# Expert layers as a 3x2 by 2x3 block product in 15 products, with the order written by a list scheduler

## The chip, the cores and the metric

The kernel runs on one core of a Trainium2 chip. The core has a matrix engine, TensorE (PE in the profile; PEld is its loading of weights), and three engines for element-wise work: VectorE (DVE), ScalarE (ACT) and GpSimd (POOL). A fifth, SyncE (SP), issues transfers. The engines run side by side, each through its own instructions in their written order, and wait for one another by semaphores. Matrix results land in PSUM, eight banks of 512 fp32 values in each of 128 partitions; everything else works in SBUF.

The metric is the device time of one launch in microseconds (us), lower is better.

## The reference

A state-space block (Mamba-2) is followed by four experts whose outputs are mixed with given weights. All is fp32.

```python
# x: (4, 8, 768, 32), a: (4, 8, 768), B and C: (4, 8, 768, 16), in chunks
L = np.exp(cum[:, :, :, None] - cum[:, :, None, :]) * causal
M = np.einsum('bhin,bhjn->bhij', Cc, Bc) * L
y[:, :, sl] = einsum(M, xc) + einsum(Cc, state) * decay_to_i
state = decay_full * state + sum(Bc * xc * decay_from_j)
...
# N, D, E, F = 3072, 256, 4, 1024; x is y turned to (3072, 256)
p = domain_probs / (domain_probs.sum(-1, keepdims=True) + 1e-09)
for e in range(E):
    h = np.maximum(x @ w1[e], 0.0)
    out += p[:, e:e + 1] * (h @ w2[e])
```

By far most of the arithmetic is in the two matrix products of the experts.

## The kernel before

**Chunks and blocks.** The 3072 tokens are 24 chunks of 128. Six blocks of 512 tokens (four chunks, one of each sequence) go through the experts one after the other; the hidden units of all experts are eight steps of 512 per block, so there are 48 steps `n`. While one block is in the experts, the scans, scores and outputs of the next block's four chunks are worked in between: `decay_part` (scans on DVE, line L364), `masks` (ACT), `scores` (PE, L393), `masked` (DVE, L405), `outputs` (PE, L450 and L462; ACT copies them to `yT`), `carry` (DVE, the state).

**Seven products for eight.** In a step each layer is a 2x2 by 2x2 block product: 256 tokens x 128 inputs against 256 hidden units, computed in seven block products after Strassen and Winograd. One block product is two matmuls of 128x128 weights against 128x256 tokens; the profile shows it as four matmul records. `fmul` (L523) does the first layer, `smul` (L608) the second. Steps 0 and 1 are done plainly, eight products a layer (`plain_first` L572, `plain_second` L589). The price of seven products is sums: of weights (`sums_of`, POOL, L189 to L193, once per step and then kept in HBM as `w1_d` and `w2_d`), of tokens (`sums`, DVE, L501 to L504, once per block), of first-layer results (`snap`, an ACT copy, L530; `total`, DVE, L535), and of gated hidden values (`diff`, DVE, L552). `gated` (DVE, L545) takes the maximum with zero and multiplies by the expert's weight.

**Second-layer sums stay in PSUM.** Four banks (`acc0` to `acc3`) hold the seven products of a block and are added to over all eight steps. After the last, `keep` and `combine` turn them into the output, which `turned_out` and `leave` write. Two banks (X, Y) serve the first layer and two the attention.

**Order.** All is written out by hand: the step loop interleaves the first layer of step n with the second layer of step n-1, and puts the attention's parts between at fixed places. Loads are issued by SP, in its one queue; the stores of weight sums by POOL:

```python
def sums_of(op, part):
    if part != 1:
        nc.gpsimd.tensor_add(op(S1), op(S3), op(A22))
...
            nc.gpsimd.dma_start(out=w1_d[n], in_=wt1[n][:, S3:])
```

Of the kernel before, what the change touches and what calls it, by code (L numbers as in the profile page):

```python
# [8 lines left out]
FP32 = mybir.dt.float32  # L9
# [3 lines left out]
P = 128  # L13
NQ, NT = 4, 2


@with_exitstack
def kernel(
# [10 lines left out]

# [3 lines left out]
    E, DM, F = w1.shape  # L60
    NH = NQ * NT
    HN = P
    BLK = 512
    HB = BLK // 2
    CPB = BLK // P
# [5 lines left out]
    FH = F // 2  # L71
    JJ = FH // HB
    SPB = E * JJ
    NS = NBLK * SPB
    assert NBLK == chunks_per_seq

    def real(c):

        return c % CPB * NBLK + c // CPB

    PLAIN = 2
    A12, A22, A11, S3, S1, S2, S4 = range(7)

    const = ctx.enter_context(tc.tile_pool(name="const", bufs=1))
    load = ctx.enter_context(tc.tile_pool(name="load", bufs=3))
    wts = ctx.enter_context(tc.tile_pool(name="wts", bufs=3))
    att = ctx.enter_context(tc.tile_pool(name="att", bufs=2))
    ffn = ctx.enter_context(tc.tile_pool(name="ffn", bufs=2))
    ps_att = ctx.enter_context(tc.tile_pool(name="ps_att", bufs=2, space=bass.MemoryType.PSUM))
    ps_f = ctx.enter_context(tc.tile_pool(name="ps_f", bufs=1, space=bass.MemoryType.PSUM))  # L90
    ps_s = ctx.enter_context(tc.tile_pool(name="ps_s", bufs=1, space=bass.MemoryType.PSUM))
    ctx.enter_context(tc.manual_schedule())


    ac_d = tc.dram_tile([NCH, NH, P], FP32, name="ac_d")
    acut_d = tc.dram_tile([NCH, NH, P], FP32, name="acut_d")
    p_d = tc.dram_tile([T // P, E, P], FP32, name="p_d")
    w1_d = [tc.dram_tile([P, 4, HB], FP32, name=f"w1_d{i}") for i in range(SPB)]
    w2_d = [tc.dram_tile([P, 5 * HB], FP32, name=f"w2_d{i}") for i in range(SPB)]


    st = {}
    SPREAD = 3

    HALF = P // 2

    def turned_round(c):


        return c >= CPB and c % 2 == 1  # L110

    def load_tokens(c):
        xb = load.tile([P, W], FP32, tag="xb", name="xb", bufs=4)
        src = xbc[real(c)]
        if turned_round(c):
            nc.sync.dma_start(out=xb[:, :OBT], in_=src[:, :OBT])
            nc.sync.dma_start(out=xb[:HALF, OBT:], in_=src[HALF:, OBT:])
            nc.sync.dma_start(out=xb[HALF:, OBT:], in_=src[:HALF, OBT:])
        else:
            nc.sync.dma_start(out=xb, in_=src)  # L120
        st.setdefault(c, {})["xb"] = xb

    def load_rows(c):

        xb = load.tile([P, W], FP32, tag="xb", name="xb", bufs=4)
        nc.sync.dma_start(out=xb[:, OBT:], in_=xbc[real(c)][:, OBT:])
        st.setdefault(c, {})["xb"] = xb

    def load_rest(c):
        nc.sync.dma_start(out=st[c]["xb"][:, :OBT], in_=xbc[real(c)][:, :OBT])  # L130

    def load_decays(c):
        ab = load.tile([P, NH * P], FP32, tag="ab", name="ab")
        nc.sync.dma_start(
            out=ab, in_=acut_d[real(c)].rearrange("h s -> (h s)").partition_broadcast(P))
        st.setdefault(c, {})["ab"] = ab

    def load_heads(c):

        ah = st[c]["ah"] = load.tile([HN, P], FP32, tag="ah", name="ah", bufs=4)  # L140
# [7 lines left out]
    def load_chunk(c):  # L148
        load_tokens(c)
        load_decays(c)  # L150
        load_heads(c)

    wt1, wt2 = {}, {}

    def load_w1(n):
        e, jj = divmod(n % SPB, JJ)
        t1 = wt1[n] = wts.tile([P, 7, HB], FP32, tag="wt1", name="wt1", bufs=5)
        for k in range(2):
            w = 2 - 2 * k
            a_ = 2 if n < SPB or k else 1  # L160
            nc.sync.dma_start(
                out=t1[:, w:w + a_],
                in_=w1[e, k * P:k * P + P].rearrange("p (a f) -> p a f", a=2)[
                    :, 0:a_, jj * HB:jj * HB + HB])
        if n >= SPB:
            nc.sync.dma_start(out=t1[:, S3:], in_=w1_d[n % SPB])

    def load_w2(n):
        e, jj = divmod(n % SPB, JJ)
        t2 = wt2[n] = wts.tile([P, 7 * HB], FP32, tag="wt2", name="wt2", bufs=5)  # L170
        for i in range(2) if n < SPB else (1,):
            f = i * FH + jj * HB
            nc.sync.dma_start(
                out=t2[:, (1 - i) * 2 * HB:(2 - i) * 2 * HB].rearrange("p (j m) -> p j m", j=JJ),
                in_=w2[e, f:f + HB].rearrange("(j p) m -> p j m", p=P))
        if n >= SPB:
            nc.sync.dma_start(out=t2[:, 2 * HB:], in_=w2_d[n % SPB])

    def w2_op(n, w):

        if w < 4:
            a_, d = divmod(w, 2)
            return wt2[n][:, :4 * HB].rearrange(
                "p (a j d m) -> p a j d m", a=2, j=JJ, d=2)[:, a_, :, d]
        return wt2[n][:, w * HB:w * HB + HB].rearrange("p (j m) -> p j m", j=JJ)

    def sums_of(op, part):
        if part != 1:
            nc.gpsimd.tensor_add(op(S1), op(S3), op(A22))  # L189
            nc.gpsimd.tensor_sub(op(S2), op(S1), op(A11))  # L190
            nc.gpsimd.tensor_sub(op(S4), op(A12), op(S2))
        if part != 0:
            nc.gpsimd.tensor_sub(op(S3), op(A11), op(S3))  # L193

    def sum_w1(n, part=None):


        if n < SPB:
            sums_of(lambda w: wt1[n][:, w].rearrange("p (j m) -> p j m", j=JJ), part)
            if part != 0:  # L200
                nc.gpsimd.dma_start(out=w1_d[n], in_=wt1[n][:, S3:])

    def sum_w2(n, part=None):
        if n < SPB:
            sums_of(lambda w: w2_op(n, w), part)
            if part != 0:
                nc.gpsimd.dma_start(out=w2_d[n], in_=wt2[n][:, 2 * HB:])

    pr = const.tile([P, T // P, E], FP32, name="pr")
    a_sb = const.tile([NCH * NH // 2, 2, P], FP32, name="a_sb")  # L210

    a_q = ffn.tile([P, SPREAD, NT, P], FP32, tag="o", name="a_q", bufs=1)
    nc.gpsimd.memset(a_q[:, 0], 0.0)
    one = nc.const_aps.tensor(1.0, [P, 1])
    nc.vector.memset(a_q[:, 1:], 0.0)
    nc.scalar.dma_start(out=pr, in_=probs)
    for queue, c in ((nc.sync, slice(0, 1)), (nc.scalar, slice(1, SPREAD))):
        queue.dma_start(
            out=a_q.rearrange("(q r) c t s -> q r c (t s)", q=NQ)[:, 0, c],
            in_=a.rearrange("(i k) (q t) s -> k q i (t s)", k=NBLK, t=NT)[0][:, c])  # L220
    warm = const.tile([P, 1], FP32, name="warm")
    nc.scalar.mul(warm, one, one)
    load_rows(0)
    nc.sync.dma_start(
        out=a_sb, in_=a.rearrange("c h s -> (c h) s").rearrange("(p r) s -> p r s", r=2))
    load_rows(1)
    load_rest(0)
    load_rest(1)
    load_w1(0)
    load_tokens(2)  # L230

# [14 lines left out]

# [4 lines left out]

# [8 lines left out]

    def clip_first(engine, c):
        clip(engine, a_q[:, c].rearrange("p c t s -> p (c t s)"), own)
        engine.memset(a_q[:, c, :, 0:1], 0.0)

    clip_first(nc.vector, slice(0, 1))


# [705 lines left out]
```

## Time and profile before

| | |
|---|---|
| median of 3 runs | 638.26 us (637.63 to 638.26) |
| span of the profiled execution, first to last instruction | 636.4 us |
| PE busy | 631.9 us (99%), 3405 matmul records |
| DVE busy | 483.4 us (76%) |
| ACT busy | 119.7 us (19%) |
| POOL busy | 112.9 us (18%) |
| transfers | 121.61 MB, mean 191 GB/s |

The page gives no other time of the profiled execution than its span; the median of the runs is 1.9 us above it. A group line names the kernel's line, the engine, the operation, what it writes and reads, and its shapes; then how often, the busy time and the mean of one. A timeline line begins with the start from the span's beginning and the length, both in us; the brackets at its end give idle time before it and what ended that. Matmuls are pipelined: a record is 0.38 us long, and the next starts 0.216 us after it.

By stage, the busy time of each engine:

| stretch, us | PE | DVE | ACT | POOL |
|---|---|---|---|---|
| 0 to 13.28 (start, first chunks) | 12.15 | 9.30 | 5.99 | 9.26 |
| 13.28 to 60 | 46.72 | 37.97 | 7.53 | 36.69 |
| 60 to 160 | 100.00 | 85.47 | 19.59 | 36.81 |
| 160 to 400 | 240.00 | 186.64 | 45.00 | 17.63 |
| 400 to 631 | 231.00 | 162.54 | 40.55 | 10.46 |

### The profile page before, as it was taken

Reading aid. Unit: us, or ns where it says so; the run is one execution under the profiler, and the core shown is the slowest. Engines: PE = TensorE matmul, PEld = TensorE weight load, DVE = VectorE, ACT = ScalarE, POOL = GpSimd, SP = SyncE. Lnnn points to the kernel's source line nnn. Section 1 sums busy time; section 2 is a strip of 40 time slices with the busy share of each in tenths; the row PEclk is TensorE's granted clock in tenths of the full one; section 3 lists DMA queues with packets and bytes.
Section 4 is the critical chain, followed back from the end, with each engine's and each line's share of the span. In section 5 each row is a group of like instructions: output and inputs, shape, how many; then the busy total and the mean of one; then the engine's idle time right before and its main releaser. Section 6 shows DMA issues by size and latency. Waiting matters only on the chain.

```text
span 636.4 us, 9259 instructions
## 1 busy us (share of the span) xinstructions
PE 631.9 (99%) x3405; PEld 538.2 (85%) x3405; DVE 483.4 (76%) x810; ACT 119.7 (19%) x264; POOL 112.9 (18%) x164
## 2 busy tenths in 40 slices
PE   9999999999999999999999999999999999999997
PEld 5888888888888888888888888888888888888886
DVE  7868999887787788678687778778867677756555
ACT  4011221212111221122211221122111211111110
POOL 6788557020000002000002000000100000100001
PEclk9999999999999999999999999999999999999999
DMA  6998894745666392757284566639365644167001
GB/s 188 302 357 295 282 346 156 279 169 166 191 200 238 90 366 81 228 175 248 99 287 149 168 199 196 231 102 358 89 220 162 242 160 133 61 152 241 2 1 33
DMA packets 98513, 121.61 MB, mean 191 GB/s; under 512 B 29529, under 2 KB 81957, under 8 KB 98469
## 3 DMA queue, kind: packets, MB, share of 16 engines
q1 hardware_dynamic: 95512, 111.20, 53.7%
q0 software_dynamic: 2432, 9.50, 3.8%
q8 instruction: 27, 0.44, 0.3%
q10 hardware_dynamic: 524, 0.32, 0.2%
q14 instruction: 18, 0.14, 0.1%
HBM read 108.16 MB, written 12.83 MB: 190 GB/s over the span
## 4 chain that ended last, share of the span: by engine, by line
PE 99%; ACT 0%; DVE 0%; issue 0%
PE acc L608 44%; PE X L523 25%; PE Y L523 19%; PE acc L589 2%; PE g L393 2%; PE y L462 2%; PE X L572 1%; PE Y L572 1%; PE y L450 1%; PE t L729 1%; PE a L331 0%; PE y L428 0%; PE gp L309 0%; PE turned L655 0%; DVE o L686 0%; ACT p_sb L298 0%
## 5 line engine op out<-in xcount | busy, mean ns | idle before, releaser
L535 DVE TENSOR_TENSOR z<-Y,snap 128x512 f32<-128x512 f32 x138 | 94.6, 686 | 117.6 <-ACT snap L530 66.7
L608 PE MATMUL acc<-hT,wt 128*128 128x256 f32 x736 | 181.1, 379 | 0.0
L530 ACT COPY snap<-X 128x512 f32<-128x512 f32 x138 | 80.8, 586 | 464.2 <-PE X L523 403.5
L608 PEld LDWEIGHTS acc<-hT,wt 128*128 128x128 f32 x736 | 140.1, 190 | 18.7
L608 PE MATMUL acc<-h,wt 128*128 128x256 f32 x552 | 142.6, 381 | 0.0
L523 PE MATMUL X<-yS,wt 128*128 128x256 f32 x552 | 141.8, 380 | 0.0
L608 PEld LDWEIGHTS acc<-h,wt 128*128 128x128 f32 x552 | 104.2, 190 | 16.8 <-issue 2.3
L523 PEld LDWEIGHTS X<-yS,wt 128*128 128x128 f32 x552 | 105.0, 190 | 14.3 <-issue 0.3
L545 DVE SCALAR_TENSOR_TENSOR h<-z,gate 128x512 f32<-128x512 f32 x138 | 99.9, 724 | 3.5 <-PE acc L589 0.4
L523 PE MATMUL Y<-yT,wt 128*128 128x256 f32 x368 | 94.5, 379 | 0.0
L523 PEld LDWEIGHTS Y<-yT,wt 128*128 128x128 f32 x368 | 68.9, 190 | 10.5
L552 DVE TENSOR_TENSOR hT<-h,hT 128x512 f32<-128x512 f32 x92 | 65.2, 709 | 1.8
L552 DVE TENSOR_TENSOR hT<-h,h 128x512 f32<-128x512 f32 x92 | 65.1, 748 | 1.4
L364 DVE TENSOR_TENSOR_SCAN LT<-ab,ident 128x512 f32<-128x512 f32 x42 | 52.1, 1242 | 0.0
L523 PE MATMUL Y<-yS,wt 128*128 128x256 f32 x184 | 48.3, 385 | 0.0
L523 PE MATMUL X<-yT,wt 128*128 128x256 f32 x184 | 47.3, 379 | 0.0
L369 POOL TENSOR_TENSOR MT<-xb,LT 128x128 f32<-128x128 f32 x20 | 8.6, 428 | 205.4 <-PE Y L523 68.8
L405 DVE TENSOR_TENSOR MT<-g,LT 128x256 f32<-128x256 f32 x93 | 32.0, 415 | 11.5 <-PE g L393 11.4
L523 PEld LDWEIGHTS Y<-yS,wt 128*128 128x128 f32 x184 | 34.2, 190 | 6.4 <-issue 2.2
L523 PEld LDWEIGHTS X<-yT,wt 128*128 128x128 f32 x184 | 35.0, 190 | 4.7
L545 DVE SCALAR_TENSOR_TENSOR h<-X,gate 128x512 f32<-128x512 f32 x50 | 34.2, 684 | 5.0 <-PE X L523 3.4
L350 POOL TENSOR_TENSOR cts<-ctm,dec 128x256 f32<-128x256 f32 x20 | 14.1, 726 | 128.3 <-DVE dec L347 128.3
(103 smaller groups left out, 325.2 us busy)
## 6 DMA issues: line engine op xcount, KB each, us to landing
wt<-in_w_dram SPq DMA_DIRECT2D x112, 256.0 KB
wt<-w_d SPq DMA_DIRECT2D x40, 640.0 KB
wt<-w_d SPq DMA_DIRECT2D x40, 512.0 KB
ab<-acut_d SPq DMA_DIRECT2D x21, 512.0 KB
gate<-p_d SPq DMA_DIRECT2D x23, 256.0 KB
w_d<-wt POOLq DMA_DIRECT2D x8, 640.0 KB, 3.7
wt<-in_w_dram SPq DMA_DIRECT2D x40, 128.0 KB
w_d<-wt POOLq DMA_DIRECT2D x8, 512.0 KB, 7.7
```

What stands on the lines that cost most here:

```text
L350: nc.gpsimd.tensor_mul(cts, s["ctm"], dec.unsqueeze(1).to_broadcast([HN, NT, P]))
L364: nc.vector.tensor_tensor_scan(out=LT[:, i * w:i * w + w], data0=s["a"][i], data1=ident.rearrange("p h s -> p (h s)")[:, :w], initial=0.0, ...
L393: nc.tensor.matmul(out=g.rearrange("p t s -> p (t s)"), lhsT=s["xb"][k, OBT:OBT + P], rhs=s["ctm"][k].rearrange("p t s -> p (t s)"), start ...
L405: nc.vector.tensor_mul(s["MT"][:, h, 0:P], s["g"][q], s["LT"][:, h])
L462: nc.tensor.matmul(out=y[32 * q:32 * q + 32, t, 0:w], lhsT=s["xb"][:, h * D:h * D + D], rhs=s["MT"][:, NT * q + t, 0:w], start=(k == 0 and ...
L523: nc.tensor.matmul(out=f[bank][:, j], lhsT=wt1[n][:, w, j * P:j * P + P], rhs=rhs, start=(i in (1, 2, 5) and j == 0), stop=(j == JJ - 1), ...
L530: nc.scalar.copy(out=s, in_=first[n]["X"])
L535: nc.vector.tensor_add(z, first[n]["Y"], first[n][i])
L545: nc.vector.scalar_tensor_tensor(out=h, in0=first[n][src], scalar=0.0, in1=g.unsqueeze(1).to_broadcast([P, JJ, HB]), op0=ALU.max, op1=ALU. ...
L552: nc.vector.tensor_sub(h[o], h[x], h[y])
L572: nc.tensor.matmul(out=f[bank][:, j], lhsT=wt1[n][:, w, j * P:j * P + P], rhs=yT[k][:, i, cols], start=(i == 0 and j == 0), stop=(i == 1), ...
L608: nc.tensor.matmul(out=acc[k, u][:, half], lhsT=w2_op(n, w)[:, j], rhs=rhs[:, j], start=(begins and j == 0), stop=(n % SPB == SPB - 1 and ...
```

## The change

**The product.** A block is now 768 tokens (six chunks), so there are four. Hidden units come in 16 slices of 256, over the expert boundaries. A *group* is three slices: its first layer is a 3x2 by 2x3 block product (three slices, two halves of the 256 inputs, three pieces of 256 tokens), done in 15 block products in place of 18 (`group_first`); its second layer is 15 in place of 18 too (`group_second`). Five groups are 15 slices; the 16th is done plainly (unit "R"). Block 0 does four slices plainly and has four groups. The tables `SUMS`, `TOKENS`, and the code of `group_first`, `group_right` and `result` are the sums around the 15 products.

**Second-layer sums.** There are 15 sums and the plain slice's extra two, more than the banks hold. They live in SBUF tiles and visit PSUM two at a time (`visit`): ACT copies the pair into a bank, four matmuls (two products) add to it, ACT copies it back.

**Weight sums.** Ten per layer and group, stored in HBM in pairs, by SP, and loaded again in later blocks. They, and every sum with both inputs in SBUF, may be done by DVE or POOL; `ASIDE0` and `ASIDE1` name sums that only POOL may do, in block 0 and in the other blocks.

**Order and buffers.** Nothing after the start is written in its final order. Each piece of work is put in a `Plan` with a duration per engine, what it reads and writes; only PE's order is given (`line`: the second layer of the last unit alternates with the first layer of this one, with scores and outputs of two chunks after the first and the 14th piece). `Plan.run` then walks through time, gives each engine in turn the ready work that is most urgent, assigns the buffer, and the instructions are emitted in the order of the planned starts. It runs while the program is built; on the chip the order is fixed, and waits follow real times.

```diff
+HOP = 0.2
+LANDING = 2.2
+KEEP = 5
+NV, NW = 33, 32
+ASIDE0 = ("t67", "p", 2, 11)
+ASIDE1 = ("t67", "p", 2, 11, "d", 7, 6, 5, 8, 12, 3)
+SC, OUT = 1, 14
...
+            e = min(t, key=lambda e: t[e])
+            now = t[e]
+            best, soon = None, None
+            late = self.late = max(0.0, t["PE"] - line[head].nominal) if head < len(line) else 0.0
+            for w in waiting[e]:
+                if w.start is not None or e == "PE" and w.place != head:
+                    continue
+                ready = max([w.ready] + [
+                    n.end + (0.0 if n.by == e and e != "SP" else HOP) for n in w.needs])
+                if len(w.on) > 1 and e == "POOL":
+                    end = max(ready, now) + w.on[e]
+                    if end > w.latest + late + w.on["DVE"] - 1.0:
+                        queue = sum(x.on["DVE"] for x in waiting["DVE"]
+                                    if x.start is None and x.latest <= w.latest)
+                        if end > max(now, t["DVE"]) + queue:
+                            continue
+                if best is not None and ready <= now and w.latest >= best[0]:
+                    continue
+                when, homes = self.homed(w, max(now, ready))
+                if when is None:
+                    continue
+                if when <= now + 0.02:
+                    if best is None or w.latest < best[0]:
+                        best = w.latest, w, when, homes
+                elif soon is None or when < soon:
+                    soon = when
...
+BLOCKS = {3: (0, 0), 9: (0, 1), "b": (1, 0), 13: (1, 1), 7: (2, 0), 0: (2, 1)}
+SUMS = ((12, "b", 13), (2, "b", 7), (11, 12, 7), (5, 11, 0), (10, 3, 12), (8, 10, 9),
+        (1, 8, 0), (6, 1, 7), (14, 5, 9), (4, 3, "b"))
+TOKENS = (("e", (0, 2), (0, 0), -1), (11, "e", (1, 2), -1), ("g", (1, 2), (1, 0), -1),
+          (2, (1, 2), (0, 2), -1), (13, "g", "e", -1), (6, (0, 0), (0, 1), 1),
+          (3, 6, (0, 2), -1), (10, "e", (1, 1), -1), (14, (1, 2), 6, -1), (4, (1, 1), (0, 1), -1),
+          (1, 6, (1, 1), -1), (9, (1, 1), "g", -1))
+RIGHT = {0: (1, 0), 5: (1, 2), 7: (0, 0), 8: (1, 1), 12: "e"}
+FIRST = (7, 12, 5, 11, 0, 3, 2, 10, 6, 13, 8, 14, 4, 1, 9)
+SECOND = ((13, 2), (11, 4), (0, 7), (1, 14), (6, 9), (5, 8), (10, 12), (3,))
+PAIRS = {1: ((12, 5), (11, 2), (10, 6), (8, 14), (4, 1)),
+         2: ((2, 11), (4, 1), (14, 6), (5, 8), (10, 12))}
...
+    homes = {
+        "V": some(NV, [P, 2, FB], "v"),
+        "W": some(NW, [P, 2 * FB], "w"),
+        "bank": some(8, [P, 512], "bank", psum),
...
-    def sums_of(op, part):
-        if part != 1:
-            nc.gpsimd.tensor_add(op(S1), op(S3), op(A22))
-            nc.gpsimd.tensor_sub(op(S2), op(S1), op(A11))
-            nc.gpsimd.tensor_sub(op(S4), op(A12), op(S2))
-        if part != 0:
-            nc.gpsimd.tensor_sub(op(S3), op(A11), op(S3))
...
+
+    plan = Plan(homes)
+    line = []
+    B512, B256 = {"DVE": .73, "POOL": 1.65}, {"DVE": .42, "POOL": .78}
...
+    def dma(fn, n=1, kb=256, **kw):
+        return plan.add({"SP": .38 * n}, fn, lag=LANDING + kb / 190, **kw)
...
-    def fmul(n, i):
...
+    def product(bank, half, w, x, start):
+
         for j in range(JJ):
+            o = bank.rearrange("p (a m) -> p a m", a=2)[:, j if half is None else half]
             nc.tensor.matmul(
-                out=f[bank][:, j], lhsT=wt1[n][:, w, j * P:j * P + P], rhs=rhs,
-                start=(i in (1, 2, 5) and j == 0), stop=(j == JJ - 1), skip_group_check=True)
-
...
+    def combine(x, y, sign=1, reuse=None, name=None):
+
+        v = value("V")
+        engines = {"POOL": B512["POOL"]} if name in aside_of[0] else B512 if "bank" not in (x.kind, y.kind) else {"DVE": .7}
+        if reuse is None:
+            reuse = x if x.kind == "V" else y
+        plan.add(engines, lambda e: (on(e).tensor_add if sign > 0 else on(e).tensor_sub)(
+            flat(v), whole(x), whole(y)), reads=[x, y], writes=[v], reuse=reuse)
+        return v
...
+    def group_weights(k, g):
+
+        for l, load, half in ((1, load_w1, w1_half), (2, load_w2, w2_half)):
+            where = {}
+            for f in range(3):
+                v = value("W")
+                dma(lambda e, load=load, v=v, f=f: load(1 + 3 * g + f, v.t), part=[v])
+                for r, b in BLOCKS.items():
+                    if b[0] == f:
...
+                    where[r] = v, j
+                if (g, l, i) in stored:
+                    dma(lambda e, v=v, i=i, l=l: nc.sync.dma_start(out=v.t, in_=w_d[g, l, i]),
+                        part=[v])
...
+                for r, x, y in SUMS:
+                    plan.add(B256, lambda e, r=r, x=x, y=y, view=view: on(e).tensor_add(
+                        view(r), view(x), view(y)), reads=[where[x][0], where[y][0]],
+                        part=[where[r][0]])
+                for i, pair in enumerate(PAIRS[l]):
+                    v = where[pair[0]][0]
+                    dma(lambda e, v=v, i=i, l=l: nc.sync.dma_start(out=w_d[g, l, i], in_=v.t),
+                        reads=[v], due=lambda v=v: v.readers[-1])
+                    stored.add((g, l, i))
+            weights[k, g, "where", l] = where
+            weights[k, g, "view", l] = view
...
+    def group_first(k, g):
+
+        seq = []
+        where, view = weights[k, g, "where", 1], weights[k, g, "view", 1]
+        G = [gate_of(k, 1 + 3 * g + f) for f in range(3)]
+        h, z, s, bank = {}, {}, {}, {}
+
+        def mul(r, into=None):
+            y, at = tokens[k, r]
+            b = into or value("bank")
+            seq.append(plan.add({"PE": .863}, lambda e: product(
+                b.t, None, view(r), at(y), into is None), reads=[where[r][0], y], writes=[b]))
+            return b
+
+        def gate(f, n, x):
+            h[f, n] = gated(x, G[f], n, -1 if f == 1 else 1)
+
+        for r in FIRST:
+            if r == 7:
+                bank[7] = mul(7)
+                s[7] = snap(bank[7])
+            elif r in (12, 5):
+                s[r] = snap(mul(r))
+                if r == 5:
+                    q = combine(s[5], s[12], -1, reuse=False)
+            elif r == 11:
+                mul(11, bank[7])
+                z[2, 2] = combine(bank[7], q, reuse=q)
+                gate(2, 2, z[2, 2])
+            elif r == 0:
+                b = mul(0, seed(s[7]))
+                gate(2, 0, b)
+            elif r == 3:
+                bank[3] = mul(3)
+                s[3] = snap(bank[3])
+            elif r == 2:
+                mul(2, bank[7])
+                z[1, 2] = combine(bank[7], s[12], -1)
+                gate(1, 2, z[1, 2])
+            elif r == 10:
+                mul(10, bank[3])
+                v17 = combine(bank[3], s[12], -1)
+            elif r == 6:
+                bank[6] = mul(6)
+                s[6] = snap(bank[6])
+                t67 = combine(s[6], s[7], -1, name="t67")
+            elif r == 13:
+                mul(13, bank[7])
+                gate(1, 0, bank[7])
+            elif r == 8:
+                bank[8] = mul(8)
+                z[0, 1] = combine(bank[8], v17)
+                gate(0, 1, z[0, 1])
+            elif r == 14:
+                mul(14, bank[6])
+                f19 = combine(bank[6], s[5], -1)
+                u = combine(f19, z[0, 1], -1, reuse=z[0, 1])
+                z[0, 2] = combine(f19, s[3], -1, name="z02")
+                gate(0, 2, z[0, 2])
+            elif r == 4:
+                b = mul(4, seed(v17))
+                gate(1, 1, b)
+            elif r == 1:
+                mul(1, bank[8])
+                z[2, 1] = combine(t67, bank[8], -1)
+                gate(2, 1, z[2, 1])
+            elif r == 9:
+                b = mul(9, seed(u))
+                gate(0, 0, b)
+        return seq, h
+
+    def group_right(h):
+
+        n10, n11, n12 = h[1, 0], h[1, 1], h[1, 2]
+        T = {13: n10, 4: n11, 1: h[2, 1], 0: h[2, 0], 9: h[0, 0]}
+        T[2] = combine(n10, n12, name=2)
+        p = combine(h[2, 2], n12, name="p")
+        T[11] = combine(p, n10, reuse=False, name=11)
+        d = combine(h[2, 0], h[2, 1], -1, name="d")
+        T[7] = combine(d, T[11], name=7)
+        T[14] = combine(h[0, 0], h[0, 2], name=14)
+        T[6] = combine(h[2, 1], T[14], name=6)
+        x9 = combine(h[0, 1], h[0, 0], -1, name="x9")
+        T[5] = combine(h[2, 2], T[14], -1, name=5)
+        T[8] = combine(x9, h[2, 1], -1, name=8)
+        T[10] = combine(x9, n11, name=10)
+        T[12] = combine(p, T[10], name=12)
+        T[3] = combine(T[10], h[0, 2], -1, name=3)
+        return T
 
     kept = {}
...
+    def visit(k, house, terms, last=False):
+
+        seq = []
+        held = kept.get((k, house))
+        both = len({t[0] for t in terms}) == 2 or held is not None and held.both
+        bank = seed(held, len(house) * FB) if held is not None else value("bank", fills=both)
+        begun = held is not None
+        for which, w, view, x in terms:
+            half = house.index(which)
+            seq.append(plan.add({"PE": .863}, lambda e, half=half, view=view, x=x, begun=begun: product(
+                bank.t, half, view(), x.t, not begun), reads=[w, x], writes=[bank]))
+            begun = True
...
+        v.both = both
+        if both:
+            act(.6, lambda e: nc.scalar.copy(out=flat(v), in_=bank.t), reads=[bank], writes=[v])
...
+    def group_second(k, g, T):
+        where, view = weights[k, g, "where", 2], weights[k, g, "view", 2]
+        seq = []
+        for house in SECOND:
+            seq += visit(k, house, [
+                (r, where[r][0], lambda r=r: view(r), T[r]) for r in house])
+        return seq
...
+        def sum_(x, y, sign, o, part=False):
+
+            vs = dict.fromkeys((x[0], y[0]))
+            engines = B256 if all(v.kind != "bank" for v in vs) else {"DVE": .42}
+            plan.add(engines, lambda e: (on(e).tensor_add if sign > 0 else on(e).tensor_sub)(
+                o[1](), x[1](), y[1]()), reads=[v for v in vs if v is not o[0]],
+                **{"part" if part else "writes": [o[0]]})
...
+    units = [(k, g) for k in range(NBLK) for g in ([*range(NG), "R"] if k else range(1, NG))]
...
+        aside_of[0] = ASIDE0 if k == 0 else ASIDE1
...
+        merged = put(behind, seq)
...
+                scores(cs)
+                at[SC] = line[mark:]
...
+                outputs(cs)
+                at[OUT] = line[mark:]
...
+    done = plan.run(line, now, {"PE": now, "DVE": now - .6, "ACT": now + 1.0, "POOL": now - 2.0,
+                                "SP": now + .4})
+    for w in done:
+        w.fn(w.by)
```

## The prediction

> **What bounds the kernel now.** I read the first two parts of the page first: who is busy, and whether anything is ever slack.
>
> ```profile
> span 636.4 us, 9259 instructions
> ...
> PE 631.9 (99%) x3405; PEld 538.2 (85%) x3405; DVE 483.4 (76%) x810; ACT 119.7 (19%) x264; POOL 112.9 (18%) x164
> ...
> PE   9999999999999999999999999999999999999997
> ...
> DVE  7868999887787788678687778778867677756555
> ...
> POOL 6788557020000002000002000000100000100001
> ```
>
> TensorE (PE) is full in every slice, the first and last apart; VectorE (DVE) is nearly full in slices 5 to 7, where GpSimd (POOL) also works. Then the chain that ended last, in order of time, to see what a product costs and how the kernel ends:
>
> ```profile
> 621.83 0.86 PE Y L523 x4
> 622.69 0.86 PE X L523 x4
> 623.55 7.77 PE acc L608 x36
> ```
>
> Four matmul records are one product (two 128x128x256 matmuls, two records each): 0.863 us. In the page's groups L523 and L608 have 1288 records each, L572 and L589 64 each: 2704/4 = 676 products, 583.4 us. The products start at 13.28 and end near 632.4, with 0.9 us of transposes among the last: 618.2 us, of which 34.8 is not products. That is scores, outputs and spreads of 22 chunks, about 1.57 each, with no room left for stalls. So there are two questions: how many products go, and whether PE stays fed.
>
> The third view decides the second question. It is the timeline of POOL, then of DVE, in one stretch where both work on SBUF, and DVE again where POOL rests:
>
> ```profile
> 92.81 0.73 POOL L189 TENSOR_TENSOR wt<-wt 128x256 f32<-128x256 f32 x1
> 93.62 1.06 POOL L190 TENSOR_TENSOR wt<-wt 128x256 f32<-128x256 f32 x1
> 94.77 1.06 POOL L191 TENSOR_TENSOR wt<-wt 128x256 f32<-128x256 f32 x1
> 95.79 1.17 POOL L193 TENSOR_TENSOR wt<-wt 128x256 f32<-128x256 f32 x1
> ```
>
> ```profile
> 92.64 1.46 DVE L545 SCALAR_TENSOR_TENSOR h<-z,gate 128x512 f32<-128x512 f32 x1
> 94.03 2.35 DVE L552 TENSOR_TENSOR hT<-h,hT 128x512 f32<-128x512 f32 x2
> 96.78 0.69 DVE L535 TENSOR_TENSOR z<-Y,snap 128x512 f32<-128x512 f32 x1 [0.41 <-ACT snap L530]
> ```
>
> ```profile
> 109.08 1.41 DVE L552 TENSOR_TENSOR hT<-h,hT 128x512 f32<-128x512 f32 x2
> ```
>
> The two sums of L552 take 1.41 alone and 2.35 beside POOL; POOL's sum takes 0.73 alone and 1.06 to 1.17 beside them. Their ends alternate, about 0.55 us for DVE's turn and 0.6 for POOL's. The z sum that reads PSUM keeps its 0.69.
>
> [...] here a 128x256 sum takes 0.724 against 0.415.
>
> **PE, part by part.** New blocks of 768 tokens, four of them. A group is three 256-wide slices of hidden units: 15 products in the first layer and 15 in the second, in place of 18 and 18. 16 slices are five groups and one plain slice (12 products). Block 0 takes four slices plainly: 48 + 4 x 30 = 168. Blocks 1 to 3: 5 x 30 + 12 = 162 each. Sum 654. So 22 products go: -22 x 0.863 = -19.0 us. The product's shape, the scores and outputs (22 chunks after the start) and the start up to 13.2 are as before: 0. The end: after the last product two 0.42 sums, two turns of PE (0.45 for two transposes in the chain before), a copy (0.37) and a transfer, as now, but one DVE sum more in a row: +0.5. Base: 636.4 - 19.0 + 0.5 = 617.9 of span; the median stands 1.9 over the span, so 619.8 if nothing stalls.
>
> **ACT.** Second-layer sums now leave PSUM after each visit and return: eight houses a group, a seed and a copy of 128x512 (0.586) each, 9.2 us; first layer five snaps and three seeds, 4.7. With masks and copies of two chunks (about 2.4) 16.3 of a unit's 29.1 us (30 products are 25.9, plus 2 x 1.57). Hidden behind PE as long as a bank is free: a visit is 0.59 + 1.73 + 0.59 plus hops, some 3.5 us, and eight banks share it with the first layer. The seed, a copy from SBUF into PSUM, is not in the trace: the copy the other way is its price, and ACT's spare 12 us a unit would bear it at nearly twice that. New waits: a product into a seeded bank waits for ACT, one that adds to a bank already read (11, 2, 13, 10, 14, 1) for ACT or DVE; all later products stand behind it on PE's queue. I take 0 to 4 us over the run; without the cover, 16 copies a unit at 0.59 would be 9 us a unit.
>
> **DMA.** Per group 6 loads of 256 KB, and from block 1 on 10 stored sums of 256 KB: 4 MB in 25.9 us, 155 GB/s, with two chunks (0.9 MB each) and the gates about 225; slices of the page reach 366. Stores (50 of 256 KB) move from POOL's queue, where an issue took POOL 0.6 us (16 of them), to SP's. SP issues some 600 transfers; the 522 of before took 0.51 each with their waits, so it is busy half the time. In SP's one queue a store waiting for a sum holds the loads behind it; these have one unit of lead (32 tiles hold two groups). Cost 0 to 3, I take 1 with ACT's.
>
> **DVE and POOL, the dear part.** Per group, first layer: 6 sums reading PSUM, 9 gates (4 read PSUM), 3 SBUF sums, plus t67 on POOL; second layer 13 SBUF sums, 10 forced to POOL in blocks 1 to 3 (ASIDE1), 3 in block 0 (ASIDE0). Neighbouring DVE starts are 0.61 (independent) to 0.72 apart: 0.65 taken. A 128x512 sum on POOL is not in the trace; 128x128 takes 0.413 and 128x256 0.724, so another 256 gives 1.35 (estimate; [...] twice 0.724 = 1.45 is the other end). The plan counts 1.65 for it and 0.73 for a DVE sum: averages that know nothing of turns.
>
> Blocks 1 and 2, a unit with two chunks (29.1 us): DVE 21 x 0.65 + four scans of 1.13 + eight masks of 0.33 + decay and carry 2.2 = 23.1. POOL 11 x 1.35 + 2.2 = 17.1. Turns: DVE 11 x 0.55 + 4 x 1.05 + 1 = 11.3, POOL about 15; 26 of 29 us for one lock. DVE waits whenever it comes to an SBUF sum while POOL holds the lock, roughly half of 19 times, 0.65 us: +6. So 29 of 29: just fed. Without chunks 13.7 + 11 x 0.3 = 17 of 25.9: slack. The unit after a block's end is short (21 products and two chunks, 21.4 us) and also gets the 23 output sums; scans can run early. I take +2 in each of blocks 1 and 2.
>
> From 13 us to the end of block 1's second unit: 213 products and 14 chunks, 206 us. Weight sums: five groups x 20 = 100 of 128x256. If POOL takes these, as the plan's rule has it (their due times are far), POOL has 100 x 0.69 + 28 forced x 1.35 + 15 = 122 us. DVE: 72 operations with a PSUM input 46.8, 56 masks 18.6, 30 gates 19.5, 61 free sums 39.7, 26 scans 29.5, 24 token sums and 23 output sums 16.4, the rest 15: 185.5, 90%. Turns: DVE 97, POOL 106: 203 of 206 us. At 98% neither can get its turn always when it wants it. If they lose 5 to 12% the stretch is 213 to 227 us, 7 to 21 too long, of which some 8 are absorbed once (second-layer sums are due half a unit after they can start). I take +7, ends 0 and +25. What is late then: the h and T tiles, so the products of the next unit; PE waits for DVE.
>
> Sum: 619.8 + 7 + 2 + 2 + 1 = 631.8, taken as 631.
>
> **Rivals.** *Fully hidden*: no stall over 4 us, 620 to 624. For it: DVE ran 99% full in slices 5 to 7 while PE lost nothing. Against: there POOL had 64 sums in all, here 100 and 200 larger ones. Chance 0.12. *The lock is the bound* (slower): with 11 POOL sums of 1.35 in a unit a DVE sum that just misses its turn waits the whole 1.35, not 0.65; then a chunk unit of blocks 1 and 2 needs 23.1 + 9.5 x 1.1 = 33.5 for 29.1. Six such units are +26, less some 12 caught up in the light ones, and the first stretch loses its +15: 619.8 + 15 + 14 = 648, range 639 to 660. It decides from 18.5 us of stalls on, that is 3% of the run. For it: the serial turns above; against: half of DVE's operations read PSUM and run beside POOL. Chance 0.37. *The count is wrong or the PE rate falls*: a stalled PE could be granted less clock; the page shows 9 in each slice and no stall to learn from. Chance 0.01, in the slow tail. The likeliest, partly stalled, 624 to 639, has 0.50.
>
> **From cases to numbers.** 0.2% is 1.3 us, about what this kernel's runs can tell from no change: 637.0 to 639.5 is "same". Of the likeliest case 0.03 and of the lock case 0.03 lie there: faster 0.47 + 0.12 = 0.59; same 0.06; slower 0.34 + 0.01 = 0.35. Range: 621 leaves out some 0.05 below, 651 some 0.13 above. The likeliest alone: 624 to 639.
>
> **What would show it.** Right: products still 0.86 each, four records; PE idle time near zero from 400 us on, and idle pieces of 0.3 to 3 us between 60 and 230, ended by DVE (h, T or z tiles) rather than DMA; DVE sums with SBUF inputs at a mean of 0.9 or more beside 0.69 for those with PSUM; POOL's 128x512 sums over 1.5. Wrong on the fast side: DVE means near 0.7 and PE 99% busy. Wrong on the slow side: POOL or DVE as the releaser of PE in each block up to the last, or PE waiting for ACT's seeds or for SP's loads behind a store, which I priced at 1.

## The result, and the profile after

The changed kernel takes 708.39 us (median of 4 runs, 705.92 to 710.74) against 638.25 beside it: a ratio of 1.110 (95% interval 1.107 to 1.114), 11% slower, where 631 was predicted. The first two parts of its page:

```profile
span 704.2 us, 10145 instructions
...
PE 642.7 (91%) x3323; PEld 531.3 (75%) x3323; DVE 578.1 (82%) x807; ACT 268.9 (38%) x559; POOL 440.6 (63%) x373
...
PE   9679989797889698988998988899998999999995
...
DVE  7579999999999989997985999765984797577544
...
POOL 4383488778765467755655767537645685665562
PEclk9899989899999989999999999999999999999999
```

The span is 67.8 us over before's 636.4 and 86.3 over the 617.9 that the prediction had as its base. PE's row is broken from slice 2 to slice 26 and nearly whole from there on; DVE's is full through most of the broken part. PEclk, the clock granted to PE, has 8s in it, which before had not. And the chain that ended last, which in the kernel before was nearly all PE, is now shared:

```profile
PE 39%; DVE 30%; issue 6%; SPq 2%; POOL 1%; DMA 1%; ACT 0%; DVEq 0%; ACTq 0%; POOLq 0%
```

The groups show how long the element-wise work became (the last two numbers before the second bar are busy us and mean ns):

```profile
L797 POOL TENSOR_TENSOR v<-v,v 128x512 f32<-128x512 f32 x208 | 309.4, 1507 | 172.4 <-DVE v L804 88.3
...
L797 DVE TENSOR_TENSOR v<-v,v 128x512 f32<-128x512 f32 x115 | 127.4, 1120 | 9.0 <-ACT v L779 5.6
L804 DVE SCALAR_TENSOR_TENSOR v<-bank,gate 128x512 f32<-128x512 f32 x97 | 66.0, 682 | 32.4 <-PE bank L770 31.5
L797 DVE TENSOR_TENSOR v<-bank,v 128x512 f32<-128x512 f32 x95 | 64.8, 682 | 30.1 <-PE bank L770 26.6
L804 DVE SCALAR_TENSOR_TENSOR v<-v,gate 128x512 f32<-128x512 f32 x95 | 82.5, 871 | 2.9
...
L399 DVE TENSOR_TENSOR_SCAN LT<-ab,ident 128x512 f32<-128x512 f32 x42 | 67.0, 1625 | 2.7 <-DMA ab<-acut_d 2.7
```

A sum of two SBUF tiles on DVE has a mean of 1120 ns, the same sum with one input in a PSUM bank 682. Taken one by one in the trace, the 35 SBUF sums that no POOL instruction overlaps take 0.691 us, the 51 that are overlapped for 95% of their length or more 1.451. The sums that read a bank keep 0.68 in both cases. Scans go from 1.208 alone to 1.844, gates on SBUF tiles from 0.688 to 1.049, POOL's own sum from 1.264 to 1.560. So 80 of the 115 sums met POOL, 51 of them nearly all the way.

Who PE waited for (us in total, times, longest):

```profile
PE bank L770 <- DVE v L797: 18.2, 11, 4.2
PE bank L770 <- ACT bank L784: 14.1, 9, 2.8
PE bank L770 <- DVE v L804: 11.1, 7, 3.8
PE bank L770 <- ACT A L422: 5.7, 1, 5.7
```

The second line looks like ACT, whose seeds (L784) copy a sum into a bank before products are added to it: second-layer sums at each visit, and three sums a group of the first layer, two of which DVE computes. In the same view over all engines the seeds themselves wait:

```profile
ACT bank L784 <- DVE v L797: 106.3, 37, 7.5
```

One such wait, from the timeline of PE, then of DVE:

```profile
94.20 2.07 PE L770 MATMUL bank<-Y,w 128*128 128x256 f32 x4 [2.81 <-ACT bank L784]
```

```profile
90.24 1.04 DVE L804 SCALAR_TENSOR_TENSOR v<-v,gate 128x512 f32<-128x512 f32 x1
91.20 0.94 DVE L844 TENSOR_TENSOR w<-w,w 128x256 f32<-128x256 f32 x1
92.06 0.68 DVE L797 TENSOR_TENSOR v<-bank,v 128x512 f32<-128x512 f32 x1
92.78 0.69 DVE L797 TENSOR_TENSOR v<-v,v 128x512 f32<-128x512 f32 x1
```

PE stands from 91.4. The sum that the seed needs ends on DVE at 93.47, the seed runs from 93.56 to 94.15, PE starts at 94.20. Ahead of that sum DVE did a gate and a weight sum beside POOL, 1.04 and 0.94 for some 0.69 and 0.42. Nothing is idle on DVE: it is behind.

By stage (from:to, length, then the busy us of PE, PEld, DVE, ACT and POOL, each with its count, the clock, the transfer share and GB/s):

```profile
13.20:62.00 48.80, 38.59 (x233) 29.47 (x232) 34.81 (x58) 6.86 (x23) 25.27 (x31) 0.90 0.80 269
62.00:250.00 188.00, 165.53 (x869) 131.35 (x869) 183.05 (x267) 66.50 (x147) 126.80 (x110) 0.93 0.52 169
250.00:450.00 200.00, 183.59 (x988) 152.70 (x987) 180.60 (x234) 79.24 (x164) 131.16 (x98) 0.98 0.57 176
450.00:660.00 210.00, 206.43 (x977) 179.97 (x978) 149.08 (x185) 95.09 (x180) 128.75 (x95) 0.99 0.50 149
```

The kernel before, in the second of these stretches:

```profile
62.00:250.00 188.00, 188.00 (x1027) 161.41 (x1027) 155.58 (x257) 36.40 (x80) 42.18 (x55) 1.00 0.63 214
```

From 62 to 250 us DVE is now busy 183 of 188 us while PE is idle 22.5. The product records say the rest: 2616 of them, 654 products, still 0.216 us from record to record where nothing stalls. Of the 86.3 us, 64.7 are 49 gaps of over 0.48 us between records, some 13 are 62 record intervals of 0.43 in place of 0.216 (half clock), about 4 come after the last product; small gaps make most of the rest.

### The profile page after: what moved, and what is told of

Read it like the earlier page. It is cut to its first block, busy times and chain, and to the rows that moved or that the text cites. A ratio compares the mean times of both kernels' runs of the same rounds, so it can differ in the third digit from the quotient of the medians.

```text
span 704.2 us, 10145 instructions
## 1 busy us (share of the span) xinstructions
PE 642.7 (91%) x3323; PEld 531.3 (75%) x3323; DVE 578.1 (82%) x807; ACT 268.9 (38%) x559; POOL 440.6 (63%) x373
## 4 chain that ended last, share of the span: by engine, by line
PE 39%; DVE 30%; issue 6%; SPq 2%; POOL 1%; DMA 1%; ACT 0%; DVEq 0%; ACTq 0%; POOLq 0%
PE bank L770 39%; DVE v L797 10%; DVE v L804 5%; DVE LT L399 5%; SPq L1075 2%; DVE v L1036 2%; DVE Y L868 2%; DVE MT L544 1%; DVE w L844 1%; DVE S L750 1%; DVE dec L681 1%; DVE M L753 1%; POOL v L797 1%; DMA w<-in_w_dram 0%; POOL w L844 0%
## 5 line engine op out<-in xcount | busy, mean ns | idle before, releaser
L770 PE MATMUL bank<-v,w 128*128 128x256 f32 x1780 | 436.5, 390 | 23.0 <-DVE v L804 9.6
L797 POOL TENSOR_TENSOR v<-v,v 128x512 f32<-128x512 f32 x208 | 309.4, 1507 | 172.4 <-DVE v L804 88.3
L770 PEld LDWEIGHTS bank<-v,w 128*128 128x128 f32 x1780 | 344.7, 195 | 82.1 <-DVE v L804 11.2
L770 PE MATMUL bank<-Y,w 128*128 128x256 f32 x760 | 200.3, 389 | 28.1 <-ACT bank L784 14.1
L770 PEld LDWEIGHTS bank<-Y,w 128*128 128x128 f32 x760 | 144.1, 193 | 57.3 <-DVE v L797 19.4
L784 ACT COPY bank<-v 128x512 f32<-128x512 f32 (+1 forms) x185 | 104.6, 575 | 118.5 <-DVE v L797 106.3
L991 ACT COPY v<-bank 128x512 f32<-128x512 f32 x142 | 83.1, 585 | 161.4 <-PE bank L770 160.8
L797 DVE TENSOR_TENSOR v<-v,v 128x512 f32<-128x512 f32 x115 | 127.4, 1120 | 9.0 <-ACT v L779 5.6
L804 DVE SCALAR_TENSOR_TENSOR v<-bank,gate 128x512 f32<-128x512 f32 x97 | 66.0, 682 | 32.4 <-PE bank L770 31.5
L804 DVE SCALAR_TENSOR_TENSOR v<-v,gate 128x512 f32<-128x512 f32 x95 | 82.5, 871 | 2.9
L779 ACT COPY v<-bank 128x512 f32<-128x512 f32 x95 | 55.7, 586 | 53.2 <-PE bank L770 47.3
L380 ACT ACTIVATE ctm<-xb,tmask 128x128 f32<-128x128 f32 x48 | 16.0, 392 | 34.8 <-PE bank L387 19.6
```

Source lines behind the costliest of these rows:

```text
L380: nc.scalar.mul(ctm[:, t], xb[:, OCT:OCT + P], tmask[:, t:t + 1])
L770: nc.tensor.matmul(out=o, lhsT=w[:, j], rhs=x if half is None else x[:, j], start=(start and j == 0), stop=(j == 1), skip_group_check=True)
L779: act(.6, lambda e: nc.scalar.copy(out=flat(v), in_=bank.t), reads=[bank], writes=[v])
L784: act(.6 if to > FB else .38, lambda e: nc.scalar.copy(out=bank.t[:, :to], in_=flat(v)[:, :to]), reads=[v], writes=[bank])
L797: plan.add(engines, lambda e: (on(e).tensor_add if sign > 0 else on(e).tensor_sub)(flat(v), whole(x), whole(y)), reads=[x, y], writes=[v], ...
L804: dve(.7 if x.kind == "bank" else .74, lambda e: nc.vector.scalar_tensor_tensor(out=h.t, in0=whole(x).rearrange("p (j m) -> p j m", j=JJ), ...
```

## The experiments

**What the shared turns cost.** In the first, POOL's 208 sums of 128x512 keep their place, and their waits, and take a little longer than before (0.29 + 3 x 0.52 us for 1.51), but hardly read: each is a sum of one column and three fills, and what follows gets zeros for the other 511 columns.

```diff
-op(flat(v), whole(x), whole(y))
...   # DVE keeps the line above; on POOL:
+op(flat(v)[:, :1], whole(x)[:, :1], whole(y)[:, :1])
+for _ in range(3):
+    nc.gpsimd.memset(flat(v)[:, 1:], 0.0)
```

> The order is the changed kernel's, instruction for instruction, but each of POOL's 208 sums of 128x512 is replaced by a sum of one column (which keeps its waits) and three fills of the rest with zeros, which only write SBUF; so the hidden values are wrong and POOL is busy as long as before, about 1.5 us each. Theory 1 (POOL's sums and DVE's two-SBUF-input sums exclude one another, and DVE falls behind): the mean of DVE's v<-v,v falls from 1.12 to at most 0.8 us, that of the scans from 1.62 to about 1.3, and the time from 708 to 640-660, the rest being the weight sums of the first 250 us. Rival (the planned order or the way through ACT's seeds is at fault, or POOL simply finishes late): the waits stay, over 695.

661.76 us, ratio 1.037 (1.034 to 1.040), just over the expected range; span 658.9: 45.3 us of span gone although POOL is busier than before (491 us for 441). DVE's and POOL's groups in it:

```profile
L800 DVE TENSOR_TENSOR v<-v,v 128x512 f32<-128x512 f32 x115 | 81.7, 723 | 29.9 <-ACT v L779 19.3 <-POOL v L804 6.9 <-POOL v L802 0.4
```

```profile
L804 POOL MEMSET v<- 128x511 f32 x624 | 326.2, 523 | 24.0
```

1120 ns became 723 beside as much POOL work. So it is not POOL's lateness but its reading that cost 45 us, the half clock after the stalls included. 41 us over the base remain.

The same done to POOL's 65 weight sums as well was to bring the rest:

> As e1, and POOL's 65 weight sums too are a one-column sum and three fills, so both the hidden values and the weights are wrong. Theory 1: the waits of the first 250 us go too: 622-640, DVE sums at 0.7, the clock back to 1.00 because PE no longer stands for 2 us and more. If the slow clock were a cause of its own and not a result of the stalls, it stays below 0.98. Rival: over 690.

667.89 us (1.047; 1.044 to 1.050), 6 worse than without it, where 622 to 640 was expected; the clock stays at 0.981 too. Four instructions for one weight sum make POOL's chain longer (504 us busy), and DVE then waits for it. That run mixes two effects. A cleaner one keeps the first edit and makes each of the 100 weight sums, on whichever engine, one column and one fill:

```diff
-on(e).tensor_add(view(r), view(x), view(y))
+on(e).tensor_add(view(r)[:, :, :1], view(x)[:, :, :1], view(y)[:, :, :1])
+on(e).memset(view(r)[:, :, 1:], 0.0)
```

> As e1 (POOL's sums of 128x512 replaced by fills), and each of the 100 weight sums, on the engine that had it, is a sum of one column and one fill, so it is short and hardly reads; hidden values and weights are wrong, the order is the changed kernel's. If what e1 left (some 25 us of waits from 62 to 250 us) is the work of the weight sums on two engines that are both full there, the time falls from 662 to 632-645, what stays being the late loads before 62 us. If it is the way from PE over ACT and DVE back to PE, it stays above 655.

647.05 us (1.014; 1.011 to 1.017), 2 over the expected range, span 645.4. The stretch from 62 to 250 us with the first edit, then with both:

```profile
62.00:250.00 188.00, 176.58 (x1032) 145.27 (x1031) 167.35 (x290) 74.50 (x164) 148.00 (x271) 0.98 0.54 174
```

```profile
62.00:250.00 188.00, 184.11 (x1062) 154.59 (x1059) 168.12 (x342) 81.56 (x177) 143.39 (x341) 0.99 0.61 196
```

PE's idle time there falls from 22.5 (changed kernel) over 11.4 (first edit) to 3.9. So the weight sums, in the one stage that has them, are another 13.5 us, their work on DVE and their reading on POOL taken together. What stays over the base, 27.5, is 9.3 of idle before 62 us, some 7 of later gaps, some 4 of half clock, some 4 after the last product, and smaller pieces.

The same question put to the kernel before, whose PE has no time to spare: from its second block on, five sums of 128x512 a step on a POOL that has little else to do there, and in a second kernel fifteen fills in their place.

```diff
+if n >= SPB:
+    nc.gpsimd.tensor_copy(pace, hid[n]["11"][:, 0, 0:1])
+    for _ in range(5):
+        nc.gpsimd.tensor_add(dum[1], dum[0], dum[0])   # or three fills
```

> The kernel before, unchanged in what it computes, with idle work for POOL: from the second block on, five sums of 128x512 of a constant tile in each of the 40 steps of 12.1 us, some 56% of POOL's time, that nobody waits for. Theory 1 (the shared turns alone): DVE's sums h<-h and gates h<-z go from 0.69 to about 1.1 in those steps, DVE from 76% to over 90% busy, and PE waits for DVE in the steps that also have scans: 641 to 660. Rival (turns cost DVE little when it has a quarter of its time free): 638, DVE means below 0.8.

> The same as b1, with three fills of 128x512 with zeros, which read nothing, in place of each sum; POOL is as busy. Theory 1: no change, 637 to 639, DVE means at 0.69. If any work of POOL slows DVE, it is as b1.

676.19 (1.060; 1.058 to 1.062) with the sums, more than expected, 659.28 (1.034; 1.032 to 1.037) with the fills. One group of each, sums first:

```profile
L555 DVE TENSOR_TENSOR hT<-h,hT 128x512 f32<-128x512 f32 x92 | 99.4, 1081 | 1.8
```

```profile
L555 DVE TENSOR_TENSOR hT<-h,hT 128x512 f32<-128x512 f32 x92 | 65.1, 708 | 1.8
```

Fills leave DVE's durations where they were (708 ns, DVE busy 483.6 us, 483.4 before), sums lift those of this group to 1081 (DVE busy 567.6). Not all groups are lifted: the other sums, `hT<-h,h`, keep 755 (748 before) and the gates of `z` 750 (724), less than expected. Who PE waited for, with the sums and with the fills:

```profile
PE Y L526 <- DVE z L538: 17.5, 13, 1.6
```

```profile
PE acc L611 <- DVE o L640: 10.2, 4, 2.6
PE acc L611 <- DVE o L642: 3.8, 1, 3.8
```

That the fills still cost 21 us was not expected: PE waited 14.0 us for output sums on DVE at the ends of blocks, where the kernel's own output sums on POOL stood behind the fills in its queue. With the sums, which keep POOL busy 256 us for the fills' 315, these waits are 1.8 us. So the 17 us between the two are the least that the reading costs, in a kernel whose DVE had a quarter of its time free.

**What half clock costs.** The kernel before with ten pauses of PE put in, each a chain of ACT copies and a small matmul that waits for it: six copies in one kernel (3.7 us), three in the other (1.8).

```diff
+if n >= 10 and n % 4 == 2:
+    src = first[n][1].rearrange("p j m -> p (j m)")
+    for i in range(6):   # or 3
+        nc.scalar.copy(out=dum[i % 2], in_=src)
+        src = dum[i % 2]
...
+    nc.tensor.matmul(out=w_, lhsT=src[:, 0:P], rhs=src[:, 0:P], start=True, stop=True)
```

> The kernel before with ten pauses of PE, one in every fourth step from step 10 on: PE waits for a chain of six ACT copies, some 3.5 us each time. Theory 2 (PE's granted clock falls to one half for some us after PE has stood for over 2 us): 10 x 3.5 for the waits and 10 x 1.7 to 3.4 for the slow products, 690 to 710, with intervals of 0.43 us between the matmul records after each pause. Rival (the slow clock in the changed kernel comes from something else, power or the higher load of the other engines): the waits alone, 670 to 676, clock 1.00.

> As c1 with chains of three copies, pauses of about 1.4 us. Theory 2 with a threshold between 1.4 and 2.3 us: the waits alone, 650 to 655, clock 1.00. If each pause costs the clock, 665 to 690.

694.74 (1.090; 1.088 to 1.091) and 660.72 (1.036; 1.034 to 1.037). Span and clock of the core, long pauses first:

```profile
core 0: 692.5 us, clock 0.978
```

```profile
core 0: 658.8 us, clock 1.000
```

Short pauses cost 22.6 us: 18 of pause, which were 1.8 us long where 1.4 was expected, and 4.6 for the extra matmuls and hops. Long ones cost 56.6: 37, the same 4.6, and 15.0 that is left. The clock record explains them: at eight of the ten pauses the granted clock is exactly 0.5, seven times for 3.4 us and once for 6.8, so 30.6 us at half rate, up to 15.3 lost (of the last, 1.6 us fall in the pause itself). In the changed kernel ten such windows, each of 3.4 or 6.8 us and 47.8 in all, begin in or after pauses of 1.9 to 5.8 us; four other pauses of 1.9 to 2.4 us have none. So pauses from 1.9 us on were enough in some cases, and two of 3.7 us were not.

**Can a better order save it?** If POOL's turns are the cost, the sums can go to DVE, or the planner can be told. First all 512-wide sums on DVE with the plan's own durations; then with the durations of undisturbed instructions:

```diff
-ASIDE0 = ("t67", "p", 2, 11)
-ASIDE1 = ("t67", "p", 2, 11, "d", 7, 6, 5, 8, 12, 3)
+ASIDE0 = ()
+ASIDE1 = ()
...
-B512, B256 = {"DVE": .73, "POOL": 1.65}, {"DVE": .42, "POOL": .78}
+B512, B256 = {"DVE": .66}, {"DVE": .36, "POOL": 1.0}   # first kernel: {"DVE": .73}, {"DVE": .42, "POOL": .78}
...
```

> All sums of 128x512 may only go to DVE (no sum is set aside for POOL); POOL keeps the weight and output sums that the scheduler gives it. Everything else, the planner's durations too, is the changed kernel's. DVE gets 208 sums more. Theory 1: each costs 0.65 and saves a turn of 1.2 to DVE's neighbours, so DVE is not busier than the 578 us of the changed kernel by more than 50 us, and the time falls to 640-670. Rival (POOL's help is needed, the lock costs little): DVE's 480 us of planned work grow to over 610, time over 720.

> As e2, with the planner's durations set to what the kernel before shows for undisturbed starts: 0.66 for sums and gates (0.64 from PSUM), 0.34 for masks, 1.15 for scans, and 1.0 for a weight sum on POOL. Theory 1: 625-645, since DVE's work alone is 566 us of 629. If DVE's total is the bound whatever the engine, it is as e2.

690.02 (1.081; 1.076 to 1.086) and 677.49 (1.062; 1.058 to 1.066). Both are slower than the theory of turns alone gave. They are better than with POOL, so the turns cost more than POOL carried, but DVE alone is then busy 595 and 597 us, and PE waits for it all the same.

Then a planner that knows turns: in the plan each instruction that reads two SBUF tiles holds `port`, the plan's name for the turn, for a set time (0.56 us for a 128x512 sum on DVE, 1.25 on POOL), and the next starts after it.

```diff
+if w.hold.get(e):
+    when = max(when, self.port)
...
+if w.hold.get(e):
+    self.port = when + w.hold[e]
```

> The same work on the same engines (the sums set aside for POOL stay so), but the planner knows the turns: it counts undisturbed lengths (0.66 for a sum on DVE, 1.38 on POOL) and gives an operation of DVE with two SBUF inputs and any operation of POOL the port one after the other (0.56 and 1.25 us for sums of 128x512). Theory 1 in its strong form (the port has more work than time while the weight sums last, so no order helps): 675 to 700. Rival (only the order was wrong, since the planner took DVE for faster than it is): below 655.

> As e4, and all sums of 128x512 on DVE, none on POOL, which keeps weight and output sums. A turn of 1.25 becomes one of 0.56, the port's load falls by some 140 us. Theory 1: 655 to 670, against e3's 677 with the same engines and a planner without turns. If the engine matters little and the order much: as e4.

683.44 (1.071; 1.068 to 1.074) with the same sums set aside for POOL, 25 us better than the change as made, and within what was expected if no order helps enough. The free sums the planner divided anew: POOL has 222 wide sums and 93 weight sums here, 208 and 65 in the changed kernel, so the 25 us are not the order's alone. 674.28 (1.057; 1.054 to 1.060) with the wide sums on DVE, a little over what was expected. Last, the loads, because the first 62 us had moved least in the runs so far. There, in the changed kernel, PE stood 6.1 us for ACT's copy `A` (L422), behind masks (L380) whose inputs landed at 24.97 us: SP, with those loads next in its queue, had stood from 14.1 to 18.0 for the store of `p_d`. A second 4.2 us was a gate on DVE behind `dec` (L681), which waited for a load. So the plan is given 3.5 us for a landing, and the gate's load 5 us later.

```diff
-LANDING = 2.2
+LANDING = 3.5
...
-        ... part=[g0])
+        ... part=[g0]).ready = now + 5.0
```

> As e5, with loads planned later: 3.5 us in place of 2.2 to land, and the load of the first expert weights 5 us later, when what it reads has been stored; so fewer instructions stand behind a load that is late. Theory 3 (some 10 us of the stalls before 62 us are late loads at the head of ACT's and DVE's queues): PE's busy time from 13.2 to 62 us rises by 4 to 8 us, and the run is 4 to 8 us shorter than e5. Rival (PE would wait there anyway, for DVE): no change of over 2 us.

664.24 (1.041; 1.038 to 1.044), 10.0 less than without it. In the stretch from 13 to 62 us the waits of ACT and DVE for transfers go from 24.1 to 7.9 us, but PE's idle time only from 6.9 to 4.4, less than expected; the rest came later, where the new plan differs too, so not all of the 10 is shown to be the loads'. It is the best version of the 15-product kernel that leaves nothing out, and still slower than the kernel before. DVE is busy 581.8 of its 662.4 us.

## Why the prediction was wrong

How late PE was against its own work done back to back, in us, just before the first group and at the end of four stretches (worked out from the start of each product in the trace, to within some 2 us; the ideal is scaled so that the end agrees with the span over the base, less what comes after the last product):

| products done | place | changed | POOL's wide sums as fills | weight sums light too |
|---|---|---|---|---|
| 46 | end of the plain part, 75 us | 17 | 20 | 18 |
| 212 | block 1's second unit | 59 | 37 | 24 |
| 323 | end of block 1 | 69 | 37 | 23 |
| 485 | end of block 2 | 82 | 37 | 23 |
| 653 | end | 82 | 36 | 23 |

- **PE, part by part: right.** 654 products at the old price; the 19.0 us are saved and then lost.
- **"From 13 us to the end of block 1's second unit": +7 taken, +25 as the end, 59 measured, 42 of them after the start.** This is the step that failed. Its mechanism was right: DVE and POOL take turns (DVE's sum of two SBUF tiles goes from 0.691 to 1.451 beside POOL), PSUM readers keep 0.68, POOL's sum alone is 1.264 (1.35 estimated) and 1.5 in company, and the late tiles are DVE's. The size was not. The step had found DVE 90% busy without waits and the turns 98% taken, and then charged a loss of 5 to 12%, with no measurement behind that share. In the trace DVE's instructions of this stretch would add up to 202 us at the mean length that each kind has where POOL is idle; they add up to 262, 30% more. 80 of 115 SBUF sums met POOL, and scans, gates, token and weight sums grew too. With 10% to spare on DVE, this ended as waits of PE. Nor was the division the one assumed: POOL was given 54 wide sums for the 28 forced ones, and DVE 35 of the 100 weight sums that were to be POOL's. Of the 42 us lost from product 46 to 212, about 25 fall with POOL's wide reads and 11 more with the weight sums (last two columns). Of the 8 us that were to be "absorbed once" nothing is seen; whether the late start had used up that lead no run isolates.
- **"I take +2 in each of blocks 1 and 2": +10 and +13 measured.** Both go to zero in the column with POOL's wide sums as fills, so both are the turns. The mean wait of a sum that met POOL, 0.62 (29 of 0.36 and 51 of 0.76), is near the 0.65 priced, but it came seven times in ten, not half the time, and the gates and scans paid too. In block 3, which has no chunks beside it, nothing more is lost, as the slack argument had it.
- **ACT and DMA, priced at 1 together: 17 by product 46, nearly all of it here.** Two instructions that waited for transfers at the head of ACT's and of DVE's queue are 10.3 us, and half clock after them, some 4, most of the rest (the stage's granted clock is 0.90). The prediction had named the danger, loads held behind a store in SP's one queue, and looked for it in the groups, not at the start. ACT itself was not late: its seeds waited for DVE.
- **The end: +0.5 taken, about +4.4 measured.** From the last product to the end are 8.4 us against 4.0 before; twelve stores stand in SP's queue there, issued from 696.4 to 702.0.
- **The rival of the clock, at 0.01: priced too low.** The clock did fall after stalls: ten windows at 0.5, 47.8 us in all. It is not a cause of its own, but it makes a long stall dearer: some 13 us in all.
- **The lock as the bound**, the lock being the turns above, was the right rival, in mechanism and sign, and at 648 (639 to 660) still 60 us short. Its terms, +15 for the first stretch and +14 for blocks 1 and 2, measured 42 and 23; the late start, 17, was not in it.
- **A reading behind the rival "fully hidden"**: DVE was not 99% full in slices 5 to 7 of the kernel before. A 9 of the page is 90% or more, and the trace gives 44.3 of 47.7 us, 93%, so that stretch said less of a full DVE than was read from it.

What stays open is whether some order makes 15 products pay. The planned-turns kernels say that division, order and loads together were worth 44 us of the 70, without reaching the kernel before; no run has the weight sums' results without their cost.

## What to carry to other kernels

Treat the turns that DVE and POOL take as an engine of its own: add up its load stage by stage, and don't let a plan with average durations fill it while either side feeds the critical engine. Before a sum is moved to POOL, ask what DVE reads meanwhile: beside POOL, DVE's sums with a PSUM input kept their 0.68 us here, those of two SBUF tiles went from 0.691 to 1.451, and beside mere fills on POOL `hT<-h,hT` kept its 708 ns. A saving on a full engine (3% of PE here) is only worth what its feeders have left, and a stall is to be priced with the slow clock that may follow it: of the changed kernel's 14 pauses of 1.9 us or more, ten had 3.4 or 6.8 us at half clock in them or after them.

## What the runs showed of the hardware

- Fifteen fills of 128x512 a step on POOL (0.525 us each) left DVE's sums of two SBUF tiles, `hT<-h,hT`, at 708 ns and the scans at 1.241 us; five sums (1.280 each) lifted them to 1081 ns and 1.880 us. Sums on POOL made these DVE instructions longer, fills did not.
- The scans and the gates (a scan or a three-input operation with two SBUF tiles) take part in the turns like plain sums: in the changed kernel they go from 1.208 to 1.844 us and from 0.688 to 1.049 where POOL works beside them.
- Pauses of 1.8 us left PE's clock whole ten times out of ten; with pauses of 3.7 us it was halved for 3.4 us or twice that at eight of ten. Between them the changed kernel shows both: windows of half clock at pauses of 1.9 and 2.0 us, and none at a pause of 2.4.
